# LSH attention with spatial gating on one core: float32 sums for two pairs, operands built by pairs, hash rows through DRAM, the bias as a product

## The chip, the core and the metric

The kernel runs on one core of a Trainium2 chip. Five engines work side by side, each with its own queue in program order: PE (TensorE, matrix products into PSUM), DVE (VectorE), ACT (ScalarE), POOL (GpSimd) and SP (SyncE), which here issues every DMA. The transfers themselves run on 16 DMA engines. The metric is the device time in microseconds; lower is better.

## The reference, cut to what matters

```python
q_bits = (q @ proj > 0); k_bits = (k @ proj > 0)          # 6 bits per row
mask   = bucket(q_bits)[:, :, :, None] == bucket(k_bits)[:, :, None, :]
scores = where(mask, q @ k.T / 8, -1e9)                   # 4 batches x 8 heads, 768 x 768
attn   = softmax(scores); x = attn @ v                    # head_dim 64
h = relu(x @ w_in); u, v = h[..., :512], h[..., 512:]
v_s = w_spatial @ layernorm(v) + b_spatial[:, None]       # mixes the 768 positions
out = (u * v_s) @ w_out
```

The results must hold to float32 accuracy. So nearly every product is made from float16 pieces: a number is split into a high half and a remainder (the "low half"), and three products (high x high, high x low, low x high) are added.

## The kernel before, in words

The 32 heads are worked in 16 pairs, four pairs to a batch. Of a pair, one load brings keys and queries transposed, both heads stacked on the 128 partitions (`qk`, 768 KB), another the values (`v`).

**Hash.** PE projects `qk` (tile `hp`), DVE turns signs into bits (`sg`), ACT scales them, and SP copies them as 12 extra rows into the operands, so that the score product itself punishes unequal hashes. The operands of a head lie in one of four `ht` tiles. Its own 64 partitions get the high half (ACT, from `cast`, 64x1536) and the remainder (DVE, L396, 64x1536); SP copies the high half to the other 64 partitions (L395); four small DMAs put the hash rows there (L401). All that is done per head, so 32 times.

**Scores, 28 heads.** For each of six query tiles: four products into `sp`; DVE copies it to `ex` (float32, 128x768) and takes the row maximum (L504); a tiny operation negates it (L507, on DVE or POOL); ACT takes the exponential (L509); the weights are split into `pp`, high half by a cast (L241 or L243, ACT or DVE), low half by a subtraction (L493, DVE or POOL); SP issues a transposing DMA to `pt` (L512); 18 small products sum into `pv` (L254, 18 float16 products of 65 or 64 columns).

**Scores, four heads** (`KHEADS` 4 to 7, that is pairs 2 and 3) are computed with the keys on the partitions and need no transpose: the row maximum comes first, from extra products (`mp`, L449), is turned by PE, and goes by a small DMA (L458) into a row of the operands. The weights `ex` are split into `pk` and summed as above.

**Normalising.** `x` is `pv` divided by its last column; it is split into `xs` and transposed by DMA into `xt` (L364), once a pair.

**Feed-forward part,** one for each batch, in units: six `vps` (with the layer norm, tile `vn`), eight `ups` (`u`), eight `sps` (the spatial product), six `ops` (output). After an `sps` unit DVE scales and adds the bias from a broadcast tile `bt` (L663), POOL multiplies by `u` (L666), ACT casts the high half of `g`, POOL subtracts for the low half (L675).

**Order.** Each step is an `op` with an engine, a cost, a sort key and the buffers it touches. `plan` goes through time with these costs and lets each free engine take the ready step of lowest key; a step with an `alt` may go to the other engine, and a locked one doesn't start while another locked one runs. The result is the order in each engine's queue; on the chip only that order and the waits hold. `RING` gives the number of buffers of each tag.

The calls all go through helpers (`matmuls`, `cast`, `lo`), so many groups share the lines L254, L241 and L493; tiles tell them apart. Weights of the feed-forward part arrive in 64-bit form (`raw`) and are converted on the way by DVE (L298 to L310) in the first third of the run.

Of the kernel before, what the change touches and what calls it, by code (L numbers as in the profile page):

```python
# [8 lines left out]
F16 = mybir.dt.float16  # L9
F32 = mybir.dt.float32  # L10
# [16 lines left out]
SW = 4096.0  # L27
HQ = 16384.0
# [4 lines left out]
def lsh_attention_spatial_gating(  # L33
# [23 lines left out]
    wk = ctx.enter_context(tc.tile_pool(name="wk", bufs=1))  # L57
    ps_sc = ctx.enter_context(tc.tile_pool(name="ps_sc", bufs=2, space=bass.MemoryType.PSUM))
# [16 lines left out]

    NHT = 4
    NR = 2 * NB
    MR = 32
    ht = [const.tile([P, 4, S], F16, name=f"ht{i}") for i in range(NHT)]

# [3 lines left out]
    bt = const.tile([P, S], F32, name="bt")  # L84
# [3 lines left out]

    RING = {"sc": 2, "pv": 2, "m": 2, "ht": NHT, "qk": 1, "v32": 1, "vp": 2, "sg0": 1, "sg1": 2,
# [15 lines left out]
    INORDER = {"sc", "ex", "pp", "pt", "pv", "ht", "qk", "vp", "v32", "xt", "xs"}  # L105
# [30 lines left out]
    def plan():  # L136


        SEM, MODE, DMA_LAT = 0.1, 0.1, 1.6
# [46 lines left out]
        while done < len(ops):  # L186
            nxt = None
            for e in free:
                while free[e] <= now:
# [33 lines left out]
                    if o.land:  # L223
                        dma = max(dma, now + DMA_LAT) + o.land
                        o.end = dma + 0.3
# [38 lines left out]
    def weights():  # L264
# [10 lines left out]
        op("SP", 0.5, 27.0, lambda: nc.sync.dma_start(out=bt, in_=b_sp.partition_broadcast(P)), w=[Bt], land=1.0)  # L275

    def job(n, src, dst, m, f, W, key):
# [5 lines left out]
        op("SP", 0.5, key - 1.5, fetch, w=[raw], land=1.6 if m == 256 else 1.1)  # L283
        if src.dtype == F32:
            wb = raw
        else:
# [19 lines left out]
            for k, e, d in ((0, "ACT", 0.33), (4, "DVE", 0.2), (1, "DVE", 0.2), (2, "DVE", 0.34), (3, "DVE", 0.34)):  # L306
                op(e, d, key - 20.0, lambda k=k: conv(k), r=[raw], w=[wb], lock=e == "DVE")
        d = 0.31 if m == 256 else 0.41
        op("ACT", d, key - 20.0, lambda eng: cast(eng, dst[0], wb.t[:, :m], f), r=[wb], w=[(W, n)], alt=("DVE", d * 0.65))
        op("DVE", 0.34 if m == 256 else 0.47, key - 20.0, lambda: nc.vector.scalar_tensor_tensor(  # L310
# [3 lines left out]
    KHEADS = (4, 5, 6, 7)  # L314
    xts = {}
    spoilt = [[False, False] for _ in range(NHT)]
# [5 lines left out]
    def pair(p):  # L322
# [4 lines left out]
        qk, v32, vp, hp, s0, s1 = (Buf(t) for t in ("qk", "v32", "vp", "m", "sg0", "sg1"))  # L327
        op("SP", 0.9, k0 - 1.9, lambda: nc.sync.dma_start(out=tile_of(qk, wk, [P, 2, S], F32, f"qk{p}"), in_=kq[b, r]), w=[qk], land=2.4)

        def hash_():  # L330
            t = tile_of(hp, ps_m, [P, 512], F32, f"hp{p}")
            matmuls([(t[32 * j:32 * j + 32, :HS], pj, qk.t[:, 1 - j // 2, (j % 2) * HS:(j % 2 + 1) * HS],
                      True, True, (0, 32 * j)) for j in range(4)])
# [5 lines left out]
        hb = [operands(2 * p + e, qk, s1, k0) for e in range(2)]  # L339

        k1 = NT * p
        op("SP", 0.5, k1 - 3.0, lambda: nc.sync.dma_start(out=tile_of(v32, wk, [P, 2 * NT, D], F32, f"v32_{p}"), in_=v[b, r]), w=[v32], land=1.3)

        op("POOL", 0.1, k1 - 1.0, lambda: nc.gpsimd.memset(
            tile_of(vp, wk, [P, 2 * NT, 2 * D + 2], F16, f"vp{p}")[:, :, 2 * D:2 * D + 2], 1.0), w=[(vp, "1")])
        op("ACT", 0.74, k1 - 0.5, lambda eng: cast(eng, vp.t[:, :, D:2 * D], v32.t, SQ), r=[v32], w=[(vp, "h")], alt=("DVE", 0.46))
        op("DVE", 0.87, k1 + 0.6, lambda: nc.vector.scalar_tensor_tensor(
            out=vp.t[:, :, 0:D], in0=v32.t, scalar=SQ, in1=vp.t[:, :, D:2 * D], op0=ALU.mult, op1=ALU.subtract), r=[v32, (vp, "h")], w=[(vp, "l")], lock=True)
        fm = mean_v(p, v32) if 2 * p in KHEADS else None
        xs = Buf("xs")  # L350
        xt = xts[p] = Buf("xt")
        for e in range(2):
# [11 lines left out]
        op("SP", 1.4, NT * p + NT - 0.5, lambda: nc.sync.dma_start_transpose(  # L364
            out=tile_of(xt, wk, [P, 2, S], F16, f"xt{p}").rearrange("p g (i r) -> p (g i) r", r=P),
            in_=xs.t.rearrange("p g i d -> p (g i d)")), r=[xs], w=[xt], land=2.0)

    def operands(H, qk, s1, k0):
        hb = Buf("ht")
        hb.t = t = ht[H % NHT]  # L370
        own, x = halves(H)
        e = H % 2
        key = k0 + 0.5 + 1.5 * e
        first = H < NHT
        fresh = spoilt[H % NHT]

        def clear():

            if first:
                nc.gpsimd.memset(t[:, 1::2], 0.0)  # L380
                for z in (0, D):
                    nc.gpsimd.memset(t[z + MR:z + MR + 1, 1], HK)
            else:
                nc.gpsimd.memset(t[x + MR:x + MR + 1, 3], 0.0)

        if first:
            op("POOL", 1.0, key - 2.0, clear, w=[hb])
        elif fresh[x // D]:
            op("POOL", 0.5, key - 2.0, clear, w=[hb])
            fresh[x // D] = False  # L390

        op("ACT", 1.38, key, lambda eng: cast(eng, t[own, 0::3], qk.t[own], SQ), r=[qk], w=[(hb, "h")], alt=("DVE", 0.86))
        op("SP", 0.5, key + 0.1, lambda: nc.sync.dma_start(out=t[x:x + D, 0::2], in_=t[own, 0::3]), r=[(hb, "h")], w=[(hb, "d")], land=0.8)  # L395
        op("DVE", 1.67, key + 0.2, lambda: nc.vector.scalar_tensor_tensor(  # L396
# [366 lines left out]
```

## Time and profile before

| | |
|---|---|
| median of 3 runs | 745.91 us (745.02 to 747.61) |
| profiled execution, device time | 744.88 us |
| its span, first to last instruction | 743.1 us |
| mean granted PE clock | 0.929 |
| transposing DMAs of softmax weights | 168, plus 16 of `xs` |
| bytes moved by DMA | 115.09 MB |

A row of the groups reads: line, engine, operation, output<-inputs, their shapes, count | busy us, mean ns of one | idle time just before them and what ended it. A row of the slices has 40 digits, each the busy share of 1/40 of the span in tenths. A row of the timeline or of the chain reads: start us, duration us, what. SPq is SP's queue: the time that issuing a DMA took there. The DMA share of a stretch is the packet time of all transfers over 16 engines' time, and it can pass 1 because packets overlap.

### The profile page before, as it was taken

The page shows a single profiled execution, that of the slowest core. Times are in us where ns is not written, and L with a number is a line of the kernel's source. Part 1 is how long each engine was busy: PE and PEld are TensorE (multiplying, and loading weights), DVE is VectorE, ACT ScalarE, POOL GpSimd, SP SyncE. Part 2 cuts the span into 40 slices and gives each one's busy share as a digit, 9 for nine tenths or more (in the row PEclk, how much of TensorE's full clock was granted, in tenths as well). Part 3 has the DMA queues.
Part 4 walks back from the last instruction along what each step waited for, and adds up shares of the span by engine and source line. Part 5 has one row for each costly group of instructions (what it writes and reads, how often), then busy time and mean ns, then how long its engine had stood idle before and what let it go on. Part 6 is the DMA issues. An engine that isn't in the chain of part 4 may idle for free.

```text
span 743.1 us, 15556 instructions
## 1 busy us (share of the span) xinstructions
PE 599.9 (81%) x5992; PEld 358.1 (48%) x5992; DVE 546.4 (74%) x1090; ACT 448.4 (60%) x640; POOL 406.0 (55%) x330
## 2 busy tenths in 40 slices
PE   2465767686486777799989989799888898999997
PEld 0133434463343544555545556456445565644553
DVE  6899898999799998766748999668769985314200
ACT  2585664699475767586756876586566865423321
POOL 7364575526064765477654766466446666541513
PEclk9878888799599898999999999999999999999999
DMA  4698977334989959899979999799989699910011
GB/s 139 158 194 194 182 155 170 85 95 96 232 160 195 199 82 200 167 204 230 169 163 225 175 189 192 147 214 180 207 177 193 135 183 161 195 50 14 1 43 43
DMA packets 309851, 115.09 MB, mean 155 GB/s; under 512 B 292240, under 2 KB 299408, under 8 KB 309776
## 3 DMA queue, kind: packets, MB, share of 16 engines
q1 hardware_dynamic: 309776, 114.09, 78.2%
q8 instruction: 47, 0.77, 0.5%
q14 instruction: 28, 0.23, 0.1%
HBM read 27.94 MB, written 6.29 MB: 46 GB/s over the span
## 4 chain that ended last, share of the span: by engine, by line
PE 33%; DVE 27%; DMA 12%; issue 11%; POOL 8%; ACT 5%; SPq 4%; POOLq 0%; DVEq 0%; ACTq 0%
PE sps L254 9%; DMA pt<-pp 9%; PE sp L254 6%; DVE ex L504 5%; PE pv L254 4%; PE vps L254 4%; PE ops L254 4%; POOL pp L493 4%; DVE ht L396 3%; SPq L401 3%; PE ups L254 3%; DVE w L298 2%; DVE mh L449 2%; DVE w L302 2%; DVE w L304 2%
## 5 line engine op out<-in xcount | busy, mean ns | idle before, releaser
L493 POOL TENSOR_TENSOR pp<-ex,pp 128x768 f16<-128x768 f32 x129 | 228.4, 1779 | 105.8 <-ACT pp L241 60.0
L254 PE MATMUL sp<-ht 128*128 128x384 f16 x768 | 174.0, 361 | 48.8 <-DVE ex L504 35.8
L509 ACT ACTIVATE ex<-ex,nb 128x768 f32<-128x768 f32 x168 | 152.8, 926 | 65.7 <-DVE nb L507 47.8
L504 DVE TENSOR_SCALAR_CACHE_REDUCE ex<-sp 128x768 f32<-128x768 f32 x168 | 157.5, 947 | 39.8 <-PE sp L254 37.7
L254 PE MATMUL pv<-vp,pt 128*128 128x65 f16 x3024 | 127.4, 199 | 49.0 <-DMA pt<-pp 49.0
L254 PEld LDWEIGHTS <-pt 128*128 128x128 f16 x3024 | 118.6, 101 | 84.2 <-DMA pt<-pp 62.0
L254 PEld LDWEIGHTS <-ht 128*128 128x128 f16 x864 | 82.4, 105 | 136.3 <-issue 85.3
L241 ACT ACTIVATE pp<-ex 128x768 f16<-128x768 f32 x145 | 120.3, 834 | 37.1 <-DMA pt<-pp 36.1
L254 PE MATMUL sps<-ws,vn 128*128 128x384 f16 x576 | 98.4, 328 | 0.0
L254 PEld LDWEIGHTS <-vn 128*128 128x128 f16 x576 | 55.9, 98 | 36.6 <-issue 0.3
L254 PE MATMUL ups<-xt,wi 128*128 128x384 f16 x384 | 66.6, 326 | 2.0 <-ACT vr L587 2.0
L254 PE MATMUL ops<-wo,g 128*128 128x512 f16 x288 | 65.8, 379 | 1.6 <-ACT g L241 0.8
L396 DVE SCALAR_TENSOR_TENSOR ht<-qk,ht 64x1536 f16<-64x1536 f32 x32 | 63.0, 1967 | 5.1 <-ACT ht L241 3.9
L254 PE MATMUL vps<-wi,xt 128*128 128x512 f16 x288 | 65.2, 380 | 0.0
L666 POOL TENSOR_TENSOR sy<-sy,u 128x384 f32<-128x384 f32 x32 | 35.4, 1105 | 51.9 <-DVE sy L663 51.9
L663 DVE SCALAR_TENSOR_TENSOR sy<-sps,bt 128x384 f32<-128x384 f32 x32 | 17.7, 555 | 58.2 <-PE sps L254 58.1
L241 ACT ACTIVATE ht<-qk 64x1536 f16<-64x1536 f32 x27 | 39.9, 1478 | 23.6 <-DMA qk<-kq 21.7
L626 POOL TENSOR_TENSOR vn<-vy,vn 128x512 f16<-128x512 f32 x24 | 31.5, 1322 | 39.7 <-ACT vn L241 38.0
L493 DVE TENSOR_TENSOR pp<-ex,pp 128x768 f16<-128x768 f32 x39 | 45.4, 1185 | 8.4 <-ACT pp L241 8.3
L254 PEld LDWEIGHTS <-wi 128*128 128x128 f16 x384 | 36.9, 98 | 25.9 <-issue 2.5
L241 ACT ACTIVATE g<-sy 128x384 f16<-128x384 f32 x31 | 16.0, 518 | 46.1 <-POOL sy L666 46.1
L254 PEld LDWEIGHTS <-g 128*128 128x128 f16 x288 | 27.1, 98 | 33.4 <-ACT g L241 1.8
(87 smaller groups left out, 699.1 us busy)
## 6 DMA issues: line engine op xcount, KB each, us to landing
qk<-kq SPq DMA_DIRECT2D x16, 768.0 KB
v<-v SPq DMA_DIRECT2D x16, 384.0 KB
ht<-ht SPq DMA_DIRECT2D x32, 192.0 KB
out<-o SPq DMA_DIRECT2D x24, 256.0 KB
raw<-w_in SPq DMA_DIRECT2D x16, 256.0 KB
pt<-pp SPq DMA_TRANSPOSE x168
raw<-w_sp SPq DMA_DIRECT2D x12, 192.0 KB
ht<-sg SPq DMA_DIRECT2D x128, 9.0 KB
```

The source lines that it names most:

```text
L241: eng.activation(out_, in_, AF.Copy, scale=1.0 if scale is None else scale)
L254: nc.tensor.matmul(out_, lhsT=lhsT, rhs=rhs, start=start, stop=stop, **({} if pos is None else {"tile_position": pos}))
L298: nc.vector.tensor_scalar(wb.t[:, :m], wb.t[:, :m], TINY, None, op0=ALU.max)
L302: nc.vector.scalar_tensor_tensor(out=wu, in0=word[:, 1], scalar=0xC0000000, in1=wu, op0=ALU.bitwise_and, op1=ALU.bitwise_or)
L396: op("DVE", 1.67, key + 0.2, lambda: nc.vector.scalar_tensor_tensor(out=t[own, 1:3], in0=qk.t[own], scalar=SQ, in1=t[own, 0::3], op0=ALU.m ...
L401: nc.sync.dma_start(out=t[x:x + NR, 3 if j < 2 else 1, (j % 2) * HS:(j % 2 + 1) * HS], in_=s1.t[32 * j + 16 * e:32 * j + 16 * e + NR, :])
L493: op("DVE", 0.87, g, lambda eng: eng.tensor_tensor(out=dst.t[:, 1], in0=ex.t, in1=dst.t[:, 0], op=ALU.subtract), r=[ex], w=[dst], lock=Tru ...
L504: op("DVE", 0.88, g, lambda: nc.vector.tensor_scalar(tile_of(ex, wk, [P, 2, HS], F32, f"ex{H}_{i}"), ps.t[:, :, :HS], -float(2 ** 27), Non ...
L509: op("ACT", 0.83, g, lambda: nc.scalar.activation(ex.t, ex.t, AF.Exp, bias=nb.t, scale=ISQ), r=[nb], w=[ex])
L626: op("POOL", 1.11, key - EV, lambda i=i, y=y: nc.gpsimd.tensor_tensor(out=vn[1].t[:, i], in0=y.t, in1=vn[0].t[:, i], op=ALU.subtract), r=[ ...
L663: op("DVE", 0.47, key - EV, lambda: nc.vector.scalar_tensor_tensor(out=tile_of(y, wk, [P, HS], F32, f"sy{b}_{d}_{h}"), in0=ps.t[:, :HS], s ...
L666: op("POOL", 0.96, key - EV, lambda: nc.gpsimd.tensor_mul(y.t, y.t, u[h].t[:, d]), r=[(u[h], d)], w=[y], lock=True)
```

## The change

1. The heads with keys on the partitions are now 2, 3, 6, 7 (pairs 1 and 3). In both pairs (`PAIRS32`) the exponentials `ex` go into the sums as they are, in float32, against float32 values (`vf`): no cast, no subtraction, six float32 products a tile instead of 18 float16 ones.
2. Operands are built by pairs: cast and remainder once over 128 partitions into tile a, then three copies by SP (L406 and L407 from a to the second head's tile b, L408 within a), a clearing by POOL (L411) of what L407 has copied away, and hash rows.
3. The hash bits go to a DRAM tile `dr` (L417) and come back as rows (L422): two DMAs a head, each with two pieces.
4. The row maximum is kept as two float16 numbers, turned by six small products and written by ACT; DMA L458 is gone.
5. The bias is one more product in each `sps` unit (two rows of `br` against constants `cb`); DVE multiplies the sums by `u` directly, POOL's product is gone.
6. The planner has other costs for DMAs; `nb` stays on DVE, more small DVE steps are locked, weight conversions have later keys; the low halves of `vn` and `g` may go to either engine.

```diff
-    KHEADS = (4, 5, 6, 7)
+    KHEADS = (2, 3, 6, 7)
+    PAIRS32 = (1, 3)
...
-        hb = [operands(2 * p + e, qk, s1, k0) for e in range(2)]
+        hb = operands(p, qk, s1, k0)
...
+        op("ACT", 1.38, key, lambda eng: cast(eng, a[:, 0::3], qk.t, SQ), r=[qk], w=[(A, "h")], alt=("DVE", 0.86))
+        op("DVE", 1.67, key + 0.2, lambda: nc.vector.scalar_tensor_tensor(
+            out=a[:, 1:3], in0=qk.t, scalar=SQ, in1=a[:, 0::3], op0=ALU.mult, op1=ALU.subtract), r=[qk, (A, "h")], w=[(A, "l")], lock=True)
...
+        op("SP", 0.6, key + 0.2, lambda: nc.sync.dma_start(out=b[lower, 0::2], in_=a[upper, 0::3]), r=[(A, "h"), (A, "x")], w=[(B, "d")], land=0.7)
+        op("SP", 0.6, key + 0.3, lambda: nc.sync.dma_start(out=b[upper], in_=a[upper]), r=[(A, "h"), (A, "l"), (A, "x"), (A, "z")], w=[(B, "o")], land=1.4)
+        op("SP", 0.6, key + 0.4, lambda: nc.sync.dma_start(out=a[upper, 0::2], in_=a[lower, 0::3]), r=[(A, "h"), (A, "l")], w=[(A, "x")], land=0.7)
...
+            nc.gpsimd.memset(a[upper, 1::2], 0.0)
...
+        op("SP", 0.6, key, lambda: nc.sync.dma_start(out=tile_of(d, dr, [P, HS], F16, f"dr{p}"), in_=s1.t), r=[s1], w=[d], land=0.5)
...
+                for g in range(2):
+                    nc.sync.dma_start(
+                        out=ab[e].t[x:x + NR, 1 + 2 * g].rearrange("r (c k) -> r c k", c=2),
+                        in_=d.t.rearrange("(g c r) k -> g r c k", g=2, c=2)[g, 16 * e:16 * e + NR])
...
-        op("SP", 0.2, key, lambda: nc.sync.dma_start(out=hb.t[x + MR:x + MR + 1, 3, :], in_=mt.t), r=[mt], w=[hb, mrow], land=0.2)
...
+        if H // 2 in PAIRS32:
+            def sums32():
+                a = sums_of(acc, H, i)
+                pe = ex.t.rearrange("p c k -> p (c k)")
+                matmuls([(a[:, q, :], pe[:, q * P:(q + 1) * P], vp.t[:, 2 * i + e, :], i == 0 and q == 0, i == NT - 1 and q == NT - 1, None)
+                         for q in range(NT)])
...
+                matmuls([(t[:, :HS], cb, br[:, hs], True, False, None)] + [
...
-        op("POOL", 0.96, key - EV, lambda: nc.gpsimd.tensor_mul(y.t, y.t, u[h].t[:, d]), r=[(u[h], d)], w=[y], lock=True)
+        op("DVE", 0.47, key - EV, lambda: nc.vector.tensor_mul(
+            tile_of(y, wk, [P, HS], F32, f"sy{b}_{d}_{h}"), ps.t[:, :HS], u[h].t[:, d]), r=[ps, (u[h], d)], w=[y])
```

How this moves the queues, at two places. First PE at the very start of the program: what stands ahead of the first scores (`sp_0` is the first query tile of the first head, `hp` the hash of a pair, `ht` the operands). Before:

```order
L254 MATMUL hp_116<-qk_91,hc 32x384 x4
L254 LDWEIGHTS ht_80
L254 MATMUL sp_0_161<-ht_80 128x384
L254 LDWEIGHTS ht_80
L254 MATMUL sp_0_161<-ht_80 128x384
```

And now:

```order
L265 MATMUL hp_113<-qk_101,hc 32x384 x4
L265 MATMUL mp_147<-vc_139,ones 128x128
L265 MATMUL hp_165<-qk_130,hc 32x384 x4
L265 MATMUL hp_209<-qk_182,hc 32x384 x4
L265 LDWEIGHTS ht_82
L265 MATMUL sp_0_214<-ht_82 128x384
```

Before, only the first pair's hash came ahead of its scores; now the hashes of three pairs do, and a product for the value mean of pair 1.

Second, SP's queue in the middle of the run, where the operands of pair 10 are built among the transposes of the weights. Before (`ht_80` and `ht_81` are the operands of its two heads; L395 copies the high halves, L401 the hash rows):

```order
L395 DMA ht_80<-ht_80 64x2x768
L512 DMA_TRANSPOSE pt_3_4858<-pp_3_4698 128x12x128
L512 DMA_TRANSPOSE pt_4_4876<-pp_4_4796 128x12x128
L364 DMA_TRANSPOSE xt_4914<-xs_4507 128x12x128
L512 DMA_TRANSPOSE pt_5_4948<-pp_5_4811 128x12x128
L512 DMA_TRANSPOSE pt_0_4974<-pp_0_4904 128x12x128
L512 DMA_TRANSPOSE pt_1_5010<-pp_1_4937 128x12x128
L395 DMA ht_81<-ht_81 64x2x768
L512 DMA_TRANSPOSE pt_2_5054<-pp_2_4980 128x12x128
L342 DMA v_10_5089<-v 128x768
L401 DMA ht_80<-sg_10_5091 12x384 x4
L401 DMA ht_81<-sg_10_5091 12x384 x4
```

And now (`ht_82` is tile a, `ht_83` tile b; the store L417 stands one transpose further up, the copy L406 three):

```order
L407 DMA ht_83<-ht_82 64x3072
L727 DMA out<-o_4_4854 128x512
L550 DMA_TRANSPOSE pt_0_4889<-pp_0_4833 128x12x128
L422 DMA ht_83<-dr_4826 12x2x384 x2
L727 DMA out<-o_5_4923 128x512
L408 DMA ht_82<-ht_82 64x2x768
L550 DMA_TRANSPOSE pt_1_4968<-pp_1_4915 128x12x128
L550 DMA_TRANSPOSE pt_2_4978<-pp_2_4943 128x12x128
L388 DMA_TRANSPOSE xt_5010<-xs_4752 128x12x128
L422 DMA ht_82<-dr_4826 12x2x384 x2
```

Before, each of these DMAs waited for an engine's result only. Now L408 waits for the landing of L407, the last L422 for POOL's clearing behind that landing, and the first L422 for the landing of the store in DRAM.

More of the change, by code (lines that the diff above doesn't have):

```diff
@@ L224, in plan @@
                         dma = max(dma, now + DMA_LAT) + o.land
[L225 removed]
+                        o.end = dma + 0.25
                     done += 1
@@ L363, in pair @@
             normalize(H, acc, xs, nm, fm)
-        op("SP", 1.4, NT * p + NT - 0.5, lambda: nc.sync.dma_start_transpose(
+        op("SP", 1.5, NT * p + NT - 0.5, lambda: nc.sync.dma_start_transpose(
             out=tile_of(xt, wk, [P, 2, S], F16, f"xt{p}").rearrange("p g (i r) -> p (g i) r", r=P),
[L366 to L375, printed above, removed]
-        def clear():
[L379 to L396, printed above, removed]
-            out=t[own, 1:3], in0=qk.t[own], scalar=SQ, in1=t[own, 0::3], op0=ALU.mult, op1=ALU.subtract), r=[qk, (hb, "h")], w=[(hb, "l")], lock=True)
-        def rows():
-            for j in range(4):
-                nc.sync.dma_start(out=t[x:x + NR, 3 if j < 2 else 1, (j % 2) * HS:(j % 2 + 1) * HS],
-                                  in_=s1.t[32 * j + 16 * e:32 * j + 16 * e + NR, :])
-        op("SP", 0.4, k0 + 0.3, rows, r=[s1], w=[(hb, "r")], land=0.5)
-        return hb
```

152 lines of the change are left out of this document (99 added, 53 removed), and 2 rows, old and new, of the table RING.

## The prediction, made before the changed kernel was run

> **What bounds the kernel now.** I read the page first, for shares, and then cut the span into three stages, because averages mix stages with different limits.
>
> ```profile
> span 743.1 us, 15556 instructions
> PE 599.9 (81%) x5992; PEld 358.1 (48%) x5992; DVE 546.4 (74%) x1090; ACT 448.4 (60%) x640; POOL 406.0 (55%) x330
> DVE  6899898999799998766748999668769985314200
> DMA  4698977334989959899979999799989699910011
> ```
>
> DVE is mostly at 8 or 9 tenths in the first 16 slices, the DMA engines in most slices from the eleventh to the 35th; the last five slices have neither. The cuts come from the output transposes on SP's queue: that of the fifth pair and that of the last.
>
> ```profile
> 252.34 1.89 SPq L364 DMA_TRANSPOSE xt<-xs  x1
> 655.81 1.43 SPq L364 DMA_TRANSPOSE xt<-xs  x1
> core 0: us, PE busy (x) PEld busy (x) DVE busy (x) ACT busy (x) POOL busy (x), PEclk, DMA share, GB/s
> 0.00:252.00 252.00, 163.33 (x1688) 96.01 (x1689) 224.29 (x445) 159.40 (x228) 131.42 (x110) 0.84 0.74 160
> 252.00:656.00 404.00, 354.75 (x3866) 219.67 (x3866) 306.33 (x611) 266.85 (x370) 247.99 (x194) 0.97 0.97 178
> 656.00:743.00 87.00, 81.77 (x440) 42.44 (x438) 15.78 (x36) 22.11 (x43) 26.57 (x27) 1.00 0.10 32
> ```
>
> The chain of work that ended last, asked for each of the three stages in turn (the shares are of the stage):
>
> ```profile
> by line: issue 14.2%; PE sp L254 6.4%; DVE ex L504 5.8%; DVE ht L396 5.7%; DVE mh L449 5.4%; DVE w L298 5.0%; PE mp L254 4.4%; DVE w L302 4.4%; DVE w L304 4.0%; DVE wi L310 2.9%; DVE vp L347 2.4%; DMA raw<-w_in 2.3%; PE pv L254 2.3%; DMA ra
> by line: DMA pt<-pp 16.0%; issue 10.2%; PE sps L254 9.4%; POOL pp L493 6.9%; PE pv L254 6.8%; PE sp L254 6.7%; SPq L401 6.2%; DVE ex L504 5.7%; PE vps L254 3.9%; PE ops L254 3.0%; DVE ht L396 2.7%; POOL sy L666 2.2%; PE ups L254 1.9%; DVE p
> by line: PE sps L254 30.7%; PE ops L254 21.8%; PE ups L254 17.9%; PE vps L254 17.9%; POOL sy L666 2.3%; issue 1.9%; DVE sy L663 1.3%; POOLq L759 1.1%; POOL g L675 1.1%; ACT o L689 0.7%; DVEq L663 0.0%; ACTq L689 0.0%; POOLq L626 0.0%
> ```
>
> So **the front (0 to 252) is DVE's**: busy 224 of 252 us, and most named pieces are DVE lines. **The middle (252 to 656) belongs to nobody alone**: PE 88% busy, DMA share 0.97, and the chain's largest piece is the landing of the transposed weights. **The tail (656 to 743) is PE's** own work on the last batch.
>
> **Front.** The groups that the change touches (mean ns after the comma):
>
> ```profile
> L396 DVE SCALAR_TENSOR_TENSOR ht<-qk,ht 64x1536 f16<-64x1536 f32 x32 | 63.0, 1967 | 5.1 <-ACT ht L241 3.9 <-POOL ht L382 0.7
> L493 DVE TENSOR_TENSOR pk<-ex,pk 128x768 f16<-128x768 f32 x14 | 14.1, 1040 | 0.0
> L493 DVE TENSOR_TENSOR pp<-ex,pp 128x768 f16<-128x768 f32 x39 | 45.4, 1185 | 8.4 <-ACT pp L241 8.3
> L493 POOL TENSOR_TENSOR pp<-ex,pp 128x768 f16<-128x768 f32 x129 | 228.4, 1779 | 105.8 <-ACT pp L241 60.0 <-DVE pp L243 22.2 <-issue 15.5
> L666 POOL TENSOR_TENSOR sy<-sy,u 128x384 f32<-128x384 f32 x32 | 35.4, 1105 | 51.9 <-DVE sy L663 51.9
> L380 POOL MEMSET ht<- 128x1536 f16 x4 | 5.5, 1387 | 0.2
> ```
>
> Counting DVE's rows in program order up to the fifth pair's normalisation: 14 operand remainders become 7 of twice the partitions and the same 1536 elements each, so 7 x 1.97 = -13.8 us; 14 low halves of the softmax weights vanish, 14 x 1.04 = -14.6; 3 more go to POOL, -3.6; eight tiny operations for the row maximum are new, at about 0.5 us each an estimate from those beside them, +4; two value splits fewer, -3. Sum -31 of 224. What is late next? PE, for it gets the float32 sums. Their nearest row is the one float32 product of 128x128 in the trace, followed by two sets of 18 float16 products:
>
> ```profile
> 133.70 0.49 PE L254 MATMUL mp<-vc,ones 128*128 128x128 f32 x2 [1.07 <-DVE mh L449]
> 134.03 0.71 PE L254 MATMUL pv<-vp,pk 128*128 128x65 f16 x18
> 134.57 0.71 PE L254 MATMUL pv<-vp,pt 128*128 128x65 f16 x18
> L254 PEld LDWEIGHTS mp<-vc,ones 128*128 128x128 f32 x4 | 0.8, 250 | 2.1 <-DVE mh L449 1.5 <-POOL pp L493 0.6
> L254 PEld LDWEIGHTS <-pk 128*128 128x128 f16 x432 | 17.1, 101 | 7.5 <-DVE pk L493 2.4 <-POOL pk L493 2.0 <-issue 1.2
> ```
>
> 18 float16 products take 134.57 - 134.03 = 0.54 us. A float32 product holds PE for 134.03 - 133.70 = 0.33, so six take up to 2.0; they stream 65 columns instead of 128, so half of that, 1.0, is the other end. I take 1.5, between them, since the weight load (250 ns against 101) does not shrink with the columns: 24 tiles x (1.5 - 0.54) = +23 us, ends +11 and +35. All of it is in the front. PE then has 186 us of work there, 84% of the 221 that would be left if all 31 came through; the middle's PE runs at 88%. That leaves little room, so I count three quarters of the 31: **-24**.
>
> The Trainium skill, "TensorE: Matmul & The Clock Gate", section "Weight-path perf modes", says that fast weight load is off for float32, and gives a load as columns / 1.2 ns. By it six products with two loads each would be an estimate of 1.28 us, and the term +18; the trace agrees that float32 loads are the slower ones.
>
> The start is rebuilt too:
>
> ```profile
> 5.84 1.48 ACT L241 ACTIVATE ht<-qk 64x1536 f16<-64x1536 f32 x1 [3.85 <-DMA qk<-kq]
> 12.14 0.82 PE L254 MATMUL sp<-ht 128*128 128x384 f16 x2 [4.75 <-DVE ht L396]
> 17.47 4.62 DMA qk<-kq
> 31.29 1.55 SPq L512 DMA_TRANSPOSE pt<-pp  x1
> ```
>
> PE's first scores now stand behind the hashes of pairs 1 and 2, so behind two more loads of qk, each 4.6 us from issue and held by the cast and remainder of the pair ahead (1.5 + 2.0): 5.84 + 2 x (4.6 + 3.5) = 22 us instead of 12. I cost that at nothing: the first transpose was issued only at 31.3, and DVE fills the time with weight conversions that it must do anyway. If that cover fails it is +10.
>
> **Middle.** SP's queue and the landings:
>
> ```profile
> 11.10 6.25 SPq L401 DMA_DIRECT2D ht<-sg  x8
> 255.60 12.88 SPq L512 DMA_TRANSPOSE pt<-pp  x5
> 272.16 6.30 SPq L401 DMA_DIRECT2D ht<-sg  x8
> 278.57 0.45 SPq L328 DMA_DIRECT2D qk<-kq  x1
> 458.49 3.62 DMA pt<-pp
> 474.06 7.66 DMA pt<-pp
> ```
>
> - **Hash rows.** Eight issues a pair take 6.3 us of SP, and the next qk load stands behind them. After: four two-piece issues, one store to DRAM and one copy more. At 0.78 each that is 4.7; if a two-piece issue and the store cost double, 8.6. I take the first end, a DMA being one instruction: the row's 6.2% of 404 = 25 us of chain shrinks by a quarter to a third, -8.
> - **Operand remainders**, 2.7% = 11 us of chain, halved: -5. **Gating product** (POOL, 2.2% = 9 us): DVE now multiplies straight from the sums, at the 0.55 us it spent there anyway: -9.
> - **Low halves on POOL**, 161 instead of 129: 1.78 against 1.19 us for each of 32, +19 of POOL work; POOL's 28 us of chain are an eighth of its 228, so +2 to +19: I take +4, nearer the former.
> - **DMA volume.** The rows are KB per issue; below them the 25 us in which most bytes moved:
>
> ```profile
> ht<-ht SPq DMA_DIRECT2D x32, 192.0 KB
> ht<-sg SPq DMA_DIRECT2D x128, 9.0 KB
> 325.00:350.00 25.00, 23.64 (x259) 13.85 (x257) 14.33 (x29) 18.52 (x24) 19.36 (x15) 1.00 1.12 223
> ```
>
> Per pair 2 x 192 + 8 x 9 = 456 KB become 192 + 384 + 192 + 96 + 72 = 936. In 11 pairs that is 5.4 MB, at 223 GB/s 24 us of transfer. The share in the middle, 0.97, is 87% of the 1.12 that it reached, so not all of it shows: between 16% (the chain's share of landings), +4, and +24. I take +12, the half.
> - **New waits on SP.** The order on SP's queue shows them: L408 waits until L407 has been read out, and the last L422 until POOL has cleared what L407 read. Transposes queued behind stand still meanwhile, and PE waits for those. A landing takes 3.6 to 7.7 us from issue; two transposes between, 2 x 2.58, hide 5.2. At nothing to 2.5 us a wait, and two waits a pair, the 11 pairs pay 0 to 55; I take 0.5 a pair, +6, since at most places two or more issues stand between. POOL's clears (1.4 us a pair) run beside.
>
> Sum of the middle: -8 - 5 - 9 + 4 + 12 + 6 = **0**. The cast that is halved on ACT (1.48 us a pair) I cost at nothing: ACT is busy 267 of 404.
>
> **Tail.**
>
> ```profile
> 718.75 11.71 PE sps L254 x72
> ```
>
> One product of 384 columns costs 11.71 / 72 = 0.163; eight for the bias of the last batch, +1.3. POOL's product in the chain, 2.3% of 87 = -2.0. Together -1.
>
> **Sum.** The profiled execution took 744.9 (1.8 around its span): 744.9 - 24 + 0 - 1 = 720; the median shown, 745.9, is 1.0 higher, which makes 721 to 722. I say **722**.
>
> **Rivals.**
> 1. *All of the relief shows* (0.17). For: DVE, ACT and SP all lose work. Against: PE and DMA gain. Front -31, middle -8 - 5 - 9 + 4 + 4 = -14, tail -1: **700**.
> 2. *PE takes DVE's place in the front* (0.15). Float32 at 2.0 us and at the granted clock of 0.84: 35 / 0.84 = 42; 163 + 42 = 205 at a busy share of 0.88 is 233, so -19 instead of -24: **727**. Against: 65% busy now.
> 3. *The DMA engines bind* (0.12): the 24 us show in full, the waits cost 12, the front yields -18. Middle -8 - 5 - 9 + 4 + 24 + 12 = +18: **745**, no change. For: share 0.97.
> 4. *SP is held at its head* (0.16), **slower**. Both new waits miss their cover by 2.5 us in every pair: 5 x 5 = 25 in the front, which leaves -6, and +55 - 6 in the middle: 744.9 - 6 + 49 - 1 + 1 = **788**; at half the miss, 1.25 us, 748. It decides from about 1.2 us a wait on. The Trainium skill, "DMA: Bandwidth & Descriptors", section "Anatomy of one DMA — SWDGE (gpsimd) path", says that a wait is served by the issuing sequencer before dispatch and that each transfer ends with a fixed delay of about 2 us, most for a target in HBM, where the hash rows now go. SP's queue in this trace does stand in order; a store to DRAM followed by its load has no row here.
>
> **Chances.** The forecast gets 0.40. Faster by over 0.3% (what a measurement can tell from no change): nearly all of the forecast, rivals 1 and 2, a third of rival 3: 0.76. Within: 0.05. Slower: rival 4 and part of 3: 0.19. Forecast and rivals 1 to 3 lie from 700 to 745; with the open ends of float32 and start I take 697, and 756 above, which leaves out most of rival 4.
>
> **What would show it.** Front: the fifth output transpose issued near 228 instead of 252, DVE busy there near 193, six float32 products in 1.0 to 2.0 us. Middle: still about 404 us to the last transpose, L422 near 0.8 us an issue, SP free of long waits on L408 and L422 (those would be rival 4), DMA share above 1.0. Wrong outright: a fifth transpose later than 252, or a middle beyond 425.

## The result, and the profile after

| | before | after |
|---|---|---|
| median | 745.46 us | 729.0 us (720.99, 725.28, 732.72, 736.03) |
| ratio, 95% interval | | 0.9705 [0.9662, 0.9749] |
| PE work, mean granted clock | 599.9 us, 0.929 | 610.9 us, 0.968 (in the 721 us execution) |
| DVE work | 546.4 us | 455.6 us |
| moved by DMA | 115.09 MB | 122.64 MB |

Every ratio, here and below, leaves out the executions that took over 1.5% more than that kernel's shortest (here two of the four). Run again, the changed kernel gave 721.09 to 733.07; the median of all ten is 726.7. I read the profile of its 721.09 us execution against the old one's 744.88. The page, as before:

```profile
span 719.3 us, 15421 instructions
PE 610.9 (85%) x5900; PEld 368.2 (51%) x5900; DVE 455.6 (63%) x1061; ACT 410.7 (57%) x600; POOL 401.4 (56%) x308
DVE  5787887669998976556487865456379845115100
DMA  8698599858999999999999799999998998720011
```

DVE's row has lost most of its nines, those of the DMA engines have stayed. The fifth and the last output transpose, and the three stages that they cut (the columns are those of the first table of stages):

```profile
221.82 1.75 SPq L388 DMA_TRANSPOSE xt<-xs  x1
630.67 1.45 SPq L388 DMA_TRANSPOSE xt<-xs  x1
0.00:222.00 222.00, 160.86 (x1529) 104.01 (x1530) 179.05 (x423) 132.53 (x199) 108.05 (x94) 0.96 0.87 189
222.00:631.00 409.00, 365.36 (x3925) 221.41 (x3923) 260.77 (x602) 255.97 (x359) 277.37 (x198) 0.97 1.01 191
631.00:719.00 88.00, 84.63 (x450) 42.80 (x447) 15.78 (x36) 22.24 (x43) 16.00 (x16) 0.99 0.10 32
```

From 252.34 / 655.81 / 743.1 it went to 221.82 / 630.67 / 719.3: **front -30.5, middle +5.4, tail +1.3 us**. This is the short execution. In the one of 736.03 us the same two transposes were issued at 234.76 and 645.61, which makes -17.6, +7.4 and +1.3. The whole gain lies in the front; the middle lost 46 us of DVE work (306 to 261) and did not get shorter. The chain through the middle and through the tail:

```profile
by line: DMA pt<-pp 18.6%; POOL pp L531 7.7%; issue 6.7%; PE pv L265 5.2%; PE sps L265 4.8%; PE sp L265 4.4%; PE ops L265 4.3%; DVE ex L542 1.9%; POOL vn L664 1.7%; ACT ex L547 1.5%; ACT pp L252 1.5%; DMA ht<-ht 1.4%; SPq L550 1.3%; PE ups 
by line: PE sps L265 34.3%; PE ops L265 26.7%; PE ups L265 17.7%; PE vps L265 17.7%; ACT o L725 0.7%; issue 0.1%; ACTq L725 0.0%
```

In the middle SP's hash rows (6.2% before) are gone from it; the landings of transposed weights lead as before. In the tail POOL's product is gone, PE's `sps` has grown.

SP's longest waits, first of before, then of after (engine and line, what it waited for: us in total, times, longest):

```profile
SPq L691 <- ACT o L689: 79.4, 9, 45.0
SPq L512 <- POOL pp L493: 52.3, 43, 3.2
SPq L512 <- PE pv L254: 25.0, 18, 2.8
SPq L512 <- PE sp L254: 22.9, 14, 2.7
```

```profile
SPq L550 <- POOL pp L531: 105.8, 82, 4.2
SPq L727 <- ACT o L725: 82.5, 12, 46.5
...
SPq L408 <- DMA ht<-ht: 9.8, 8, 2.4
```

The transposes now wait 105.8 us for POOL's low halves instead of 52.3, but the two waits for PE, 47.9 us before, are no longer among the longest. Summed over all rows, of which most are not shown, SP's transposes of weights wait 187 us instead of 165: 171 instead of 103 for POOL and 4 instead of 54 for PE. So the freed time of SP went into waiting only in part; for the most part one wait took the place of another. The landing waits that I had feared are 9.8 us in all on L408, and 4.0 on L422 (1.6 of it for a landing, 2.4 for POOL). The rest of the weights' path, by groups (busy us, mean ns of one | idle before):

```profile
L531 POOL TENSOR_TENSOR pp<-ex,pp 128x768 f16<-128x768 f32 x161 | 270.9, 1695 | 95.9 <-ACT pp L252 39.4 <-DVE pp L254 32.8 <-issue 12.2
L401 DVE SCALAR_TENSOR_TENSOR ht<-qk,ht 128x1536 f16<-128x1536 f32 x16 | 32.5, 2029 | 1.1 <-ACT ht L252 0.9
L411 POOL MEMSET ht<- 64x1536 f16 x16 | 22.4, 1403 | 37.2 <-DMA ht<-ht 16.1 <-DMA raw<-w_in 6.8 <-DMA ht<-dr 6.6
```

And the bytes of the middle, of before and of after (the DMA view: packets and MB, then the share of 16 engines' time that the packets of SP's queue took):

```profile
DMA packets 222190, 72.00 MB, mean 178 GB/s; under 512 B 214912, under 2 KB 218080, under 8 KB 222143
q1 hardware_dynamic: 222143, 71.37, 96.2%
```

```profile
DMA packets 228390, 77.92 MB, mean 191 GB/s; under 512 B 219221, under 2 KB 223541, under 8 KB 228341
q1 hardware_dynamic: 228341, 77.26, 100.5%
```

Packet time went from 0.962 x 404 = 389 us to 1.005 x 409 = 411, for 5.9 MB more. By the view's count of issues, 4.4 MB of these are the operands of the nine pairs that are built in this stage; the rest is one load of values, one of weights and two transposes more that now fall into it.

### The profile page after: what moved, and what is told of

Its sections match the earlier page's. It is cut to its first block, busy times and chain, and to the rows that moved or that the text cites. A ratio compares the mean times of both kernels' runs of the same rounds, so it can differ in the third digit from the quotient of the medians.

```text
span 734.2 us, 15421 instructions
## 1 busy us (share of the span) xinstructions
PE 624.6 (85%) x5900; PEld 377.2 (51%) x5900; DVE 455.7 (62%) x1061; ACT 411.2 (56%) x600; POOL 400.1 (54%) x308
## 2 busy tenths in 40 slices
DMA packets 315334, 122.64 MB, mean 167 GB/s; under 512 B 295003, under 2 KB 304219, under 8 KB 315260
## 4 chain that ended last, share of the span: by engine, by line
PE 33%; DMA 25%; DVE 13%; POOL 11%; issue 9%; ACT 7%; SPq 2%; POOLq 0%; ACTq 0%; DVEq 0%
DMA pt<-pp 19%; PE pv L265 8%; POOL pp L531 8%; PE sps L265 7%; PE ops L265 6%; PE sp L265 5%; DVE ex L542 4%; PE ups L265 3%; ACT ex L547 3%; DMA qk<-kq 2%; PE vps L265 2%; DMA ht<-ht 2%; ACT pp L252 2%; DMA raw<-w_in 1%; SPq L550 1%
## 5 line engine op out<-in xcount | busy, mean ns | idle before, releaser
L531 POOL TENSOR_TENSOR pp<-ex,pp 128x768 f16<-128x768 f32 x161 | 269.2, 1684 | 98.1 <-ACT pp L252 44.5
L265 PE MATMUL sp<-ht 128*128 128x384 f16 x768 | 164.9, 347 | 24.1 <-DVE ex L542 23.1
L265 PEld LDWEIGHTS <-pt 128*128 128x128 f16 x3024 | 112.4, 99 | 91.2 <-DMA pt<-pp 73.6
L252 ACT ACTIVATE pp<-ex 128x768 f16<-128x768 f32 x135 | 111.8, 835 | 15.7 <-DMA pt<-pp 14.6
L701 DVE TENSOR_TENSOR sy<-sps,u 128x384 f32<-128x384 f32 x32 | 17.8, 557 | 80.8 <-PE sps L265 79.0
L711 POOL TENSOR_TENSOR g<-sy,g 128x384 f16<-128x384 f32 x32 | 29.5, 921 | 57.3 <-ACT g L252 56.8
L664 POOL TENSOR_TENSOR vn<-vy,vn 128x512 f16<-128x512 f32 x24 | 30.1, 1267 | 39.3 <-ACT vn L252 26.7
L265 PEld LDWEIGHTS <-xt 128*128 128x128 f16 x288 | 27.8, 99 | 32.0 <-issue 1.7
L265 PEld LDWEIGHTS pv<-vf,ex 128*128 128x128 f32 x288 | 41.4, 221 | 5.4 <-ACT ex L499 3.0
L411 POOL MEMSET ht<- 64x1536 f16 x16 | 22.3, 1393 | 38.7 <-DMA ht<-ht 24.9
L265 PE MATMUL pv<-vf,ex 128*128 128x65 f32 x288 | 41.5, 302 | 2.1 <-ACT ex L499 2.1
```

Of the source, the lines that this page charges most:

```text
L252: eng.activation(out_, in_, AF.Copy, scale=1.0 if scale is None else scale)
L265: nc.tensor.matmul(out_, lhsT=lhsT, rhs=rhs, start=start, stop=stop, **({} if pos is None else {"tile_position": pos}))
L411: nc.gpsimd.memset(a[upper, 1::2], 0.0)
L531: op("DVE", 0.87, g, lambda eng: eng.tensor_tensor(out=dst.t[:, 1], in0=ex.t, in1=dst.t[:, 0], op=ALU.subtract), r=[ex], w=[dst], lock=Tru ...
L664: op("DVE", 0.6, key - EV, lambda eng, i=i, y=y: eng.tensor_tensor(out=vn[1].t[:, i], in0=y.t, in1=vn[0].t[:, i], op=ALU.subtract), r=[y], ...
L701: op("DVE", 0.47, key - EV, lambda: nc.vector.tensor_mul(tile_of(y, wk, [P, HS], F32, f"sy{b}_{d}_{h}"), ps.t[:, :HS], u[h].t[:, d]), r=[p ...
```

## The experiments

All start from the changed kernel; "changed" is its 726.7 us. Ratios are to the kernel before, with 95% intervals. The changed kernel itself gave 0.9705 and, run again, 0.9779, which is 5.5 us apart; so a difference of some 5 us between two runs is not told apart. Medians are over all executions.

| run | median (range) | ratio |
|---|---|---|
| e1 changed kernel again | 726.66 (721.09 to 733.07) | 0.9779 [0.9737, 0.9821] |
| e2 sums in float16 | 742.59 (741.49 to 746.10) | 0.9982 [0.9957, 1.0006] |
| e3 remainder twice | 736.37 (732.07 to 745.27) | 0.9868 [0.9832, 0.9905] |
| e4 copy L407 twice | 788.86 (786.65 to 791.71) | 1.0599 [1.0566, 1.0631] |
| e5 copy planned later | 730.16 (721.55 to 736.32) | 0.9706 [0.9663, 0.9750] |
| e6 more bytes | 736.85 (728.31 to 746.61) | 0.9843 [0.9810, 0.9876] |
| e7 later loads at the start | 733.04 (725.38 to 747.09) | 0.9753 [0.9710, 0.9796] |
| e8 hash rows without DRAM | 759.26 (755.75 to 764.52) | 1.0179 [1.0139, 1.0218] |
| e9 bias as before | 725.13 (718.92 to 729.76) | 0.9718 [0.9672, 0.9764] |
| e10 clearing twice | 730.07 (726.27 to 737.19) | 0.9795 [0.9764, 0.9827] |
| e11 low halves to DVE | 726.67 (721.58 to 734.46) | 0.9725 [0.9689, 0.9760] |
| e12 more float16 products | 729.02 (727.31 to 731.94) | 0.9793 [0.9766, 0.9819] |

### e1, the same kernel again

> The changed kernel once more, for a second profile and more times. Theory (PE's clock decides between its times of 721 and 736): the profile whose granted clock is higher is the shorter one; the stretch of float32 sums of pair 3 (in the first profile 155 to 176 us at half clock) then runs at full clock, about 9 us shorter, and the fifth output transpose is issued near 225 instead of 235. Rival (the DMA queue decides): the stretch is the same in both and the difference lies behind 235 us.

726.66 us, and the theory holds for this pair of profiles: the one with the higher clock (0.968 against 0.950) is the shorter, the stretch of pair 3 runs at full clock in it, and the fifth output transpose was issued at 221.8 instead of 234.8. Its profile is the one read above; the stretch is shown in the last section.

### e2, the two pairs' sums in float16 again

```diff
-    PAIRS32 = (1, 3)
+    PAIRS32 = ()
```

> Pairs 1 and 3 keep their keys on the partitions, but their weights are again split into two float16 halves and summed by 18 products; all else as changed. Theory (the float32 sums relieve DVE, POOL and ACT in the front, and that was worth more than PE's extra): the first stage gets 24 casts and 24 subtractions back, about 20 us of ACT and 25 to 40 us of DVE and POOL; 8 to 15 us slower than the changed kernel, 731 to 738. Rival (float32 costs as much as it saves: 24 x 0.75 = 18 us of PE, and a cold clock): equal or up to 8 us faster, 715 to 723, with PE at full clock from 140 to 180 us.

742.59 us: **the float32 sums are worth 16 us** in the medians, more than the 8 to 15 expected, and without them the rest of the change, taken together, is worth next to nothing. Its front and middle:

```profile
0.00:245.00 245.00, 159.58 (x1693) 93.50 (x1694) 202.19 (x426) 148.75 (x221) 136.89 (x108) 0.87 0.80 172
245.00:651.00 406.00, 364.95 (x3903) 220.14 (x3901) 257.73 (x609) 255.21 (x360) 282.92 (x204) 0.97 1.02 191
```

The front is 23.7 us longer than in e1 (to the fifth output transpose, 245.54 against 221.82) and has 23 us more of DVE; the middle is as long as ever.

### e3, the operand remainder computed twice

```diff
-        op("DVE", 1.67, key + 0.2, lambda: nc.vector.scalar_tensor_tensor(
+        op("DVE", 1.67, key + 0.2, lambda: [nc.vector.scalar_tensor_tensor(
...
-            ...), r=[qk, (A, "h")], w=[(A, "l")], lock=True)
+            ...) for _ in range(2)], r=[qk, (A, "h")], w=[(A, "l")], lock=True)
```

> The operands' remainder on DVE is computed twice (the same result), 16 x 2.1 = 34 us more of DVE, order of all else unchanged. Theory (DVE no longer binds, at 62% busy): +3 to +10 us. Rival (DVE still binds the front and every us counts): 7 of the 16 lie in the front, +14 us there, +20 to +34 in all.

736.37 us: 33 us of added remainders (their group takes 65.7 us instead of 32.5) cost 10, about a third, by the ratios 7 to 12. Its front and middle:

```profile
0.00:233.00 233.00, 167.55 (x1530) 106.97 (x1531) 188.46 (x430) 132.41 (x199) 110.61 (x94) 0.92 0.84 180
233.00:645.00 412.00, 361.81 (x3920) 219.61 (x3919) 273.85 (x611) 255.95 (x359) 283.88 (x198) 0.98 1.01 189
```

Seven of the 16 lie in the front, and there the fifth output transpose comes 10.9 us later than in e1 (232.75); the middle is 3.8 us longer. Some of the 10.9 is no cost of DVE: in e6, e7, e10, e11 and e12, where DVE's work in the front is at most 1 us above e1's, it comes 2 to 6 us later too.

### e4, the copy L407 issued twice; e5, the planner told that it lands 3 us later; e6, another load in its place

```diff
-        op("SP", 0.6, key + 0.3, lambda: nc.sync.dma_start(out=b[upper], in_=a[upper]), ...
+        op("SP", 0.6, key + 0.3, lambda: [nc.sync.dma_start(out=b[upper], in_=a[upper]) for _ in range(2)], ...
```

> The copy of 384 KB from the first to the second head's operands is issued twice (same bytes), 6.3 MB more, 16 issues more on SP, order unchanged. Theory (the DMA engines bind the middle now, share 1.03): at 200 GB/s 31 us of transfer, of which two thirds show, +18 to +30. Rival (the transfer hides, PE binds): +0 to +8.

In e5 the planner takes that step to end 3 us later, so the order moves its readers back:

```diff
-                        o.end = dma + 0.25
+                        o.end = dma + 0.25 + o.lag
...
-        op("SP", 0.6, key + 0.3, ..., w=[(B, "o")], land=1.4)
+        op("SP", 0.6, key + 0.3, ..., w=[(B, "o")], land=1.4, lag=3.0)
```

> The planner is told that the copy to the second head's operands lands 3 us later than it assumed, so the copy and the hash rows that wait for that landing stand further down in SP's queue; the work is the same. Theory (a landing waited for at the head of SP's queue costs its length one for one; the changed kernel has some 15 us of such waits): 8 to 15 us faster than the changed kernel, 710 to 718, and no wait of SP for that landing. Rival (there SP has slack, since it waits for POOL 118 us): within 4 us, 720 to 728.

In e6 each pair's L407 is followed by one more load of 384 KB into a tile that nobody reads:

```diff
...
+                                          nc.sync.dma_start(out=spare, in_=kq[bb, rr, :, 0])], r=...
```

> One more load of 384 KB a pair into a tile that nobody reads, behind the copy to the second head's operands: 6.3 MB and 16 issues more, as in the doubled copy, but nothing waits for it. Theory (the doubled copy's +63 us was its wait of 4.2 us a pair, and volume costs less): 10 to 25 us over the changed kernel, 735 to 750. Rival (volume alone did it, the DMA engines bind): +50 or more, 775 to 790.

e4 cost 62 us, more than theory and rival had allowed, and its SP waits say why:

```profile
SPq L407 <- DMA ht<-ht: 66.8, 16, 6.6
```

The second copy writes what the first writes, so it stands at SP's head until the first has landed, 4.2 us a pair, with all transposes behind it. In the front these waits are 30.1 us and the front is 31.1 us longer than in e1; in the middle 36.7, and it is 34.5 us longer. So a landing wait there costs its length nearly one for one. The bytes are not to blame for most of it: e6 moves as many more and costs 10 us in the median (5 to 10 by the ratios), 7 from shortest to shortest. Its middle has 3.7 MB more than e1's and is 1.7 us longer:

```profile
DMA packets 229998, 81.61 MB, mean 199 GB/s; under 512 B 219634, under 2 KB 223954, under 8 KB 229949
```

In e5 the waits of L408 and L422 are not among SP's eleven longest any more, and the time is the changed kernel's, as the rival said: those waits were covered.

### e7, pair 2's loads held until the second query tile

```diff
+    first = Buf()
...
-        op("SP", 0.6, k0 - 1.9, lambda: nc.sync.dma_start(out=tile_of(qk, ...), in_=kq[b, r]), w=[qk], land=2.4)
+        op("SP", 0.6, k0 - 1.9, lambda: nc.sync.dma_start(out=tile_of(qk, ...), in_=kq[b, r]), r=[first] if p == 2 else [], w=[qk], land=2.4)
```

(`v` the same; the product of that tile writes `first`.)

> The loads of pair 2 (keys, queries, values), and so its hash, are held until the second query tile of the first head is in PE. Theory (the start costs the changed kernel some 6 us, because the first scores stand behind the third load): first scores near 24 instead of 30 us, 3 to 7 us faster, 719 to 723. Rival (the front's length is set behind the start, by DVE and PE): first scores earlier, the fifth transpose not, within 3 us.

733.04 us, not told apart from the changed kernel. The first scores came at 21.8 us instead of 26.2 in e1, but the first transpose of weights was issued at 34.1 instead of 33.9. The first output transpose came at 69.5 us instead of 72.4, the second at 105.9 instead of 99.9, the fifth at 226.6 instead of 221.8. A miss for the idea that the late start counts, though no clean test of it: the edit also brings pair 2 later.

### e8, hash rows straight from SBUF, four DMAs a head, no store

```diff
-        op("SP", 0.6, key, lambda: nc.sync.dma_start(out=tile_of(d, dr, ...), in_=s1.t), r=[s1], w=[d], land=0.5)
+        op("SP", 0.6, key, lambda: None, r=[s1], w=[d], land=0.5)
...
-                for g in range(2):
-                    nc.sync.dma_start(out=ab[e].t[x:x + NR, 1 + 2 * g]..., in_=d.t...)
+                for j in range(4):
+                    nc.sync.dma_start(out=ab[e].t[x:x + NR, 1 + 2 * (j // 2), (j % 2) * HS:(j % 2 + 1) * HS],
+                                      in_=s1.t[32 * j + 16 * e:32 * j + 16 * e + NR, :])
```

> The hash rows go straight from the SBUF tile to the operands by 128 small DMAs, as before the change, instead of 16 stores to DRAM and 64 DMAs back: 48 issues more at 0.63 to 0.8 us, 30 to 38 us more of SP. Theory (SP's issue time is on the chain, a quarter to a third of it shows): +8 to +15, 734 to 741. Rival (SP has slack now): within 4 us.

759.26 us, 33 more: over twice what the theory allowed. The fifth output transpose stands at 230.2 (8.4 later than in e1), the last at 669.1, so the middle is 438.9 us, 30 longer:

```profile
230.00:669.00 439.00, 376.67 (x3883) 226.00 (x3882) 256.64 (x601) 254.60 (x355) 276.32 (x200) 0.92 0.94 177
```

The hash rows of one pair on SP's queue, then such rows of e1 (start, time spent issuing):

```profile
265.12 3.52 SPq L422 DMA_DIRECT2D ht<-sg  x4
283.49 3.83 SPq L422 DMA_DIRECT2D ht<-sg  x4
```

```profile
277.20 1.40 SPq L422 DMA_DIRECT2D ht<-dr  x2
291.62 1.27 SPq L422 DMA_DIRECT2D ht<-dr  x2
319.24 1.15 SPq L417 DMA_DIRECT2D dr<-sg  x1
```

In e8's middle there are 72 such issues instead of 36 and 9 stores. Summed over all of them, SP spends 56 us on them against 25 in e1: 31 us of issue time, and in this stage it shows in full. In the front it does not: 46 us against 21 there, and 8.4 us of the 25 show. The share of the DMA engines in the middle falls to 0.94, as it should if SP hands out their work late.

### e9, the bias as before

```diff
-                matmuls([(t[:, :HS], cb, br[:, hs], True, False, None)] + [
...
+            op("DVE", 0.47, key - EV, lambda: nc.vector.scalar_tensor_tensor(
+                out=tile_of(y, ...), in0=ps.t[:, :HS], scalar=1.0 / (SN * SW), in1=bt[:, hs], op0=ALU.mult, op1=ALU.add), r=[ps, Bt], w=[y])
+            op("POOL", 0.96, key - EV, lambda: nc.gpsimd.tensor_mul(y.t, y.t, u[h].t[:, d]), r=[(u[h], d)], w=[y], lock=True)
```

> The bias goes back to what it was: broadcast tile, DVE scales and adds, POOL multiplies by u; the product row is gone. By the prediction's terms (-9 us in the middle, -1 us in the tail for the bias as a product) the time is some 10 us above the changed kernel, near 737 us, with the middle near 418 instead of 409 to 411 us. Rival: POOL's product lay beside other work, so nothing is lost, 724 to 730 us; in the tail POOL's product comes back for 2 us while eight products of 0.16 us leave PE.

725.13 us: nothing lost, the rival's answer. POOL's 26 us more (427 instead of 401) lay beside other work. The tail from the last output transpose (640.70 of a 727.9 us span) is 87.2 us instead of 88.6.

### e10, tile a cleared twice

```diff
             nc.gpsimd.memset(a[upper, 1::2], 0.0)
+            nc.gpsimd.memset(a[upper, 1::2], 0.0)
```

> The clearing of tile a is done twice, 16 more memsets of about 1.4 us on POOL (+22 us of its 400) and the last hash rows of each pair wait 1.4 us longer for it. If POOL and its clear give back what the rows through DRAM won, a third to all of the 22 us shows: 734 to 749 us, and the time lies in the middle. Rival: the copies have slack (as the run with the later copy showed) and POOL has idle time, so 725 to 731 us.

730.07 us: 3 us for 22 of POOL work, within what two such medians differ by. In its profile the middle is 414.0 us, 5 longer, with 14 us more of POOL there. So POOL's total is not by itself what holds the middle; that a part of it shows is not excluded.

### e11, 73 low halves from POOL to DVE

```diff
-        WEIGH = {"DVE": 1.8, "ACT": 1.0, "POOL": 0.6}
+        WEIGH = {"DVE": 1.8, "ACT": 1.0, "POOL": 0.98}
```

> The planner weighs POOL dearer, which brings 73 of the 161 low halves of softmax weights from POOL to DVE (80 on DVE, 88 on POOL): POOL -123 us of work, DVE +87. If POOL's late low halves (118 us of SP's wait in the profile of the changed kernel, 12% of the middle's chain) hold the transposes, the middle shortens by 5 to 15 us: 712 to 722 us. Rival: SP waits for whichever is last, the chain goes to DVE, and the front, where DVE is at 76%, grows: 727 to 740 us.

726.67 us, no change. The planner moved more than the 73: POOL's total fell from 401 to 229 us, since low halves of `xs`, `vn` and `g` went to DVE too. SP's waits moved to the next engine:

```profile
SPq L550 <- POOL pp L531: 39.8, 28, 4.2
SPq L550 <- PE sp L265: 37.7, 29, 2.4
SPq L550 <- PE pv L265: 24.9, 18, 2.8
```

```profile
228.00:631.00 403.00, 362.58 (x3905) 219.93 (x3898) 309.53 (x688) 255.34 (x352) 149.16 (x110) 0.97 1.03 194
```

The wait for POOL fell from 105.8 to 39.8 us and 62.6 us of waiting for PE came up. POOL lost 128 us in the middle (277 to 149), and the stage is 403 instead of 409. The front gave that back, as the rival said: the fifth output transpose stands at 227.7, 5.9 us later.

### e12, two score products more in each float32 tile

```diff
+            if H // 2 in PAIRS32:
+                matmuls([(t[:, c, :HS], hb.t[:, 0, at], hb.t[:, 1, c * HS:(c + 1) * HS], True, True, None) for c in range(2)])
             products(t, hb.t, 0, 1, at)
```

> In the tiles of the two float32 pairs two of the four score products are issued once more ahead of the four (48 more float16 products of 384 columns, 8 us of PE work at full clock; they are overwritten). If the half clock in the second float32 stage comes from float32 products being too thin a load to bring the clock back, that stage now stays near full clock in every run: the spread shrinks from 15 us to below 8, the median is 722 to 728 us, and the stage between the third and fourth output transposes takes about 42 us. Rival: the extra work simply adds, 730 to 738 us, with the spread and an occasional half-clock stretch as before.

729.02 us, and the six times lie within 4.6 us where the changed kernel's ten lie within 15. The third and fourth output transposes stand 42.5 us apart (135.41 and 177.93). Both are as the theory said; the median is not, it is no better than without the products. It trades the long executions for the short ones, in these six.

## Why the prediction was right

It said 722; the median is 729.0 (726.7 over ten), inside the range, with the sign and the place of the gain (front) right, and e2 shows that the float32 sums carry it, as forecast. In the middle the total came out near zero by luck. By its steps:

- **Front, -24.** Measured -30.5 in the 721 us execution and -17.6 in the 736 us one (three quarters of the 31 would be 23, not 24). The float32 price lies inside its ends: six products from 84.66 to 85.95 are 1.29 us at full clock, where I took 1.5. PE's added work is then 24 x (1.29 - 0.54) = 18 us. The prediction's estimate of 1.28 from the Trainium skill's page "TensorE: Matmul & The Clock Gate" was the closer one (the columns / 1.2 ns stand in its section "LDWEIGHTS (loading the stationary operand)"); the trace agrees with the sum at full clock, and whether the weight loads set that pace no run separated.

```profile
84.66 1.45 PE L265 MATMUL pv<-vf,ex 128*128 128x65 f32 x12
85.95 0.81 PE L265 MATMUL sp<-ht 128*128 128x384 f16 x4
```

  Yet PE's busy time in the front did not rise to the 186 us of the prediction: it went from 163 to 161, while its granted clock went from 0.84 to 0.96. Busy time times clock is 137 and 154, a rough estimate of the work at full clock, and there the +17 to 18 are. That the clock would pay for them was not in the prediction; why it rose is not shown, but e2, with float16 sums, has 0.87. DVE's relief was sized too small: 224 went to 179, not to 193. Part of it is in the weight conversions, which I had left as they were and which took less each in the new order (one of their groups, in the front of before and of after):

```profile
L298 DVE TENSOR_SCALAR w<-w 128x256 f32<-128x256 f32 x23 | 16.1, 708 | 4.3 <-ACT w L294 4.2
```

```profile
L315 DVE TENSOR_SCALAR w<-w 128x256 f32<-128x256 f32 x22 | 12.6, 575 | 3.4 <-ACT w L311 3.2
```

  Without the float32 sums (e2) the front gains 6.8 us instead of 30.5.
- **Start, nothing.** The front's length shows nothing of it, though the first scores came at 26.2 us in the 721 us execution and 29.9 in the other, not at 22: the first transpose of weights was issued at 33.9 and 37.8 instead of 31.3, and in e7 earlier scores brought no earlier transpose.
- **Middle, 0.** Measured +5.4, but from parts of another size. e8 divides it: with the hash rows as before the change, the middle of the changed kernel is 438.9 us, 35 more than before, and the rows through DRAM take 30 off. The prediction had +8 and -8, so two errors of opposite sign cancelled.
  - *Hash rows, -8*: mis-sized. I took the cost from the chain's share, 25 us, cut by a third. Yet the 72 issues that before had in this stage took 56 us of the queue that hands out every transpose, against 25 for 36 issues and 9 stores now, and in this stage e8 shows that time one for one. (The third copy of the operands takes back 5.5.)
  - *Gating product, -9*: 0 by e9, the same misreading the other way: its share of the chain was not what its removal brought.
  - *Low halves on POOL, +4*: e11 takes them off POOL for 5 us of the stage and nothing in the median.
  - *New SP waits, +6*: 0 by e5.
  - *Operand remainders, -5*: e3's middle is 3.8 us longer (412.7), with as much DVE work added as had been saved.
  - *DMA volume, +12*: packet time rose by 22 us, near the upper end, but little of it shows: by e6, whose middle is 1.7 us longer for 3.7 MB and whose median is 10 us up for 6.3 MB, +3 to +9 for 5.9 MB. The prediction's bytes came out by luck: it counted eleven pairs in this stage, where its own seven in the front leave nine, and other transfers made up for it.
- **What is left open.** Of the 35 us these terms explain some 15 at most; some 20 have no run that names them. e11 shows the form of it: SP, once free, waits for POOL, and with POOL relieved for PE, which is busy 365 of 409 us; and the DMA engines' share is 1.01 to 1.04 in this stage in all changed kernels but e4 and e8. The stage takes 403 to 415 us in all kernels, the one before among them, but e4 and e8, while time added to SP's queue there comes through. That fits several limits that lie close together, which is an argument and not a measurement. Whether PE or the landings end last there, no run separated.
- **Tail, -1.** Measured +1.3: the product is +1.3 as worked out, POOL's -2.0 did not come, though no POOL is left in the tail's chain: PE was behind it. e9, with POOL's product back and the bias product gone, has 87.2 us, as the kernel before (87.3).
- **Rivals.** The fourth named a real mechanism: e4 is it, at full price. It lacked its cause here, since the order leaves room behind each copy. (The section cited with it is about DMAs that GpSimd issues; here SP issues all.) The third's DMA engines are near their limit, without the loss. The second had float32 at a lower clock; the longer executions show it in one stretch (below), but in the front as a whole the clock rose. That its 727 is the median of ten is a coincidence.

## What to carry to other kernels

Price a step on an issuing queue by all the time that it takes there, not by its share of the chain: where that queue feeds the bound, added issue time or a landing wait at its head shows one for one (here in the middle; in the front a third of the added issue time showed). A piece's share of the chain is not what its removal brings: the gating product's 9 us were worth nothing here. Where several engines are near their limit, moving work between them can do no more than change who is waited for, as in e11. Going through DRAM paid here since it saved issues, not transfers. Read the clock beside an engine's busy time: here the same busy time held 17 us more of work.

## What the hardware showed that was not expected

PE's granted clock can stay at half for some 20 us while PE is fully busy with float32 products of 65 columns and the float16 score products between them. Two executions of the same kernel, the 736.03 us one first, then the 721.09 us one, in the stage of the second float32 pair (columns as in the tables of stages; the clock is the third figure from the end):

```profile
150.00:160.00 10.00, 8.64 (x52) 6.82 (x51) 6.30 (x13) 4.23 (x8) 2.93 (x3) 0.79 0.58 178
160.00:170.00 10.00, 10.00 (x45) 8.79 (x46) 0.56 (x1) 3.23 (x5) 0.73 (x1) 0.50 0.29 71
```

```profile
150.00:160.00 10.00, 10.00 (x85) 9.03 (x84) 4.26 (x9) 4.92 (x8) 2.39 (x3) 1.00 0.56 161
160.00:170.00 10.00, 6.62 (x55) 3.71 (x54) 9.90 (x23) 7.22 (x11) 5.14 (x5) 0.91 0.68 164
```

In the first PE is busy for all of 160 to 170 and its clock is 0.50. It fell at about 156, some 2 us after a wait of 1.36 us for an exponential; that this wait was the cause is not shown:

```profile
153.83 1.55 PE L265 MATMUL pv<-vf,ex 128*128 128x65 f32 x12 [1.36 <-ACT ex L499]
155.22 0.93 PE L265 MATMUL sp<-ht 128*128 128x384 f16 x4
155.94 2.66 PE L265 MATMUL pv<-vf,ex 128*128 128x65 f32 x12
158.39 1.48 PE L265 MATMUL sp<-ht 128*128 128x384 f16 x4
```

From there six float32 products take 158.39 - 155.94 = 2.45 us instead of 1.29, and from the third to the fourth output transpose it is 50.1 us (135.13 to 185.26) instead of 39.4 (132.32 to 171.76). That is 10.7 of the 15 us between the two executions.

The Trainium skill, "TensorE: Matmul & The Clock Gate", section "What's actually happening", has one busy window of about 3.4 us release the clock. The trace does not agree: 160 to 170 alone holds more than two of them at 0.50. Of the other profiles, e5's of 734.46 us and e9's of 729.76 us have the same stretch; e12's of 731.94 us, with more float16 work in between, does not (160 to 170, in this order):

```profile
160.00:170.00 10.00, 10.00 (x44) 8.52 (x42) 1.48 (x3) 3.21 (x5) 0.73 (x1) 0.50 0.22 62
160.00:170.00 10.00, 10.00 (x44) 8.44 (x43) 1.59 (x4) 2.44 (x4) 0.73 (x1) 0.50 0.35 78
160.00:170.00 10.00, 10.00 (x80) 7.50 (x79) 5.41 (x12) 5.38 (x9) 2.22 (x3) 1.00 0.62 162
```

Half clock for as long also occurs with float16 work, at 236.5 to 257 in the 721 us execution, but PE is busy only two thirds of that time. That float32 products are too thin a load to bring the clock back fits all of this, and so does e12's narrow spread; one profile and six times of e12 do not show it.
